# Attention and ReGLU feed-forward on one core: one queue for batch 0's loads, weight rounding on GpSimd alone, and a shorter wait for the value products

## The chip and the metric

One NeuronCore of a Trainium2 chip runs the whole kernel. The time is the device time of one execution in microseconds. Before the change the median of three runs is 424.37 us (424.24 to 425.08). A profile is one further execution, recorded instruction by instruction. TensorE (PE) multiplies matrices, VectorE (DVE), ScalarE (ACT) and GpSimd (POOL) work elementwise, and SyncE (SP) only issues transfers. Each engine runs its own instructions in order, and semaphores hold an instruction until what it needs is there.

## What is computed

Eight batches of eight heads, 576 query rows, 16 extra "beacon" keys in front of 576 keys, 64 elements a head. Causal softmax attention is followed by a feed-forward block with a ReLU gate over all 4608 rows:

```python
k_all = concatenate([beacon_k, k], axis=2)          # 8, 8, 592, 64
v_all = concatenate([beacon_v, v], axis=2)
scores = q @ k_all.T / 8, masked causally behind the beacons
a = exp(scores - max) / sum
x = (a @ v_all) as 4608 x 512
out = (maximum(x @ w_gate, 0) * (x @ w_val)) @ w_out  # 512 -> 1536 -> 512
```

## The kernel before

**A planner writes the order.** The kernel does not issue work in loop order. `Plan.add` (L132) collects tasks, each with an engine (or several to choose from), a modelled cost, what it depends on, which buffers it holds and a priority. `Plan.order` (L140) then simulates all engines and repeatedly starts the task that can begin earliest; ties go by priority. Only after that are the instructions emitted, in that order. So a changed cost, priority or limit can move instructions everywhere. A task that lists two engines, such as `("ACT", "DVE")`, is given to the one that could begin it first. `Hold` and `Slots` stand for buffers that are taken and given back; `Share` limits how many buffers of a common pool one kind of task may hold.

**Loads and preparation of a batch** (`new_batch`, L415). For each of the four head pairs there is one k and one q load of 512 rows (`load_pair`, L451). The remaining 64 rows of k with the 16 beacon rows, and the first 64 and the last 16 rows of q, are the *rest* pieces: one tile of 80 rows for k and one for q, each by two transfers of many short runs (`load_rest`, L487). v comes in five tiles of up to 128 rows (`load_v`, L524). Every load lands in one of `N_ST` = 7 staging tiles `st`. `rounded` (L423) casts it to bf16 into one of three tiles `h16` (L429), on POOL, or for batch 0 on POOL or DVE; `turned` (L434) transposes it on PE against the identity (L441) into PSUM; an eviction copies it on ACT (L386) or DVE (L388) into `kT` or `diag`. `diag` is a block layout of q that must be zero elsewhere: the first two batches' `diag` tiles are cleared once by `make_zeros` (L368), one on DVE and one on POOL. The letters of `ORDER0` (L541) give the order of batch 0's loads: `K` and `Q` the rest pieces, `0` to `3` the pair loads (first k, then q), `v` the v tiles. Batch 0's rest pieces are issued from ACT's queue (`ACT_B` = 1, L497 and L500), everything else from SP's.

**Attention** (`group`, L652, and `tile_step`, L556). For each pair: scores on PE (L602, L594), mask and row minimum on DVE (L617, L614; the scores carry a minus sign), exponential with row sum on ACT (L628), the reciprocal on DVE (L640), the normalisation of the bf16 weights `pa` and `pb` (L647) on POOL (batch 0: POOL or DVE). The weights are then transposed into `pTa` and `pTb`: on PE for batch 0 (L685), by transfers of SP's queue otherwise (L695). The value products (L706, L728) write two PSUM tiles a pair and group, which are copied to `xT`. The scores of batch b are not planned before `PACE` = 39 us times b.

**Values in runs.** The value matmuls use halves or quarters of PE's array, and the planner charges `SWITCH` for going in and out of that mode (`part=True`). Their task carries `lazy` (L734): as long as PE is not in the mode and fewer than `LAZY` us have passed since the product was ready, other PE work that could begin at the same time goes first (L178). So several products gather into one run.

**PSUM banks.** Eight banks are shared (L306 to L308). Scores may hold `SC_MOST` = 4 of them, the feed-forward block `F_MOST` = 3, and values together with the turns of batch 1 and later `V_MOST` = 4.

**Weights.** 36 tiles of 128x512 f32 (12 of each matrix) are loaded by SP into `osb` staging tiles (L401; a pool of `N_OSB` = 6 that the output uses later) and rounded to bf16 by the engine that the planner picks out of `WCAST`, POOL (L390) or ACT (L386).

**Feed-forward** (`ffn`, L755). Spans of 240, 336, then 512 rows and a last one of 448: twelve blocks of a gate product (L764), ReLU on ACT (L775), a value product (L769) and the multiplication on DVE (L779); then the output product in three parts (L792), a copy to `osb` and a store by SP (L802). It needs the `xT` rows of its span and the weights, and fills PE wherever attention leaves room.

Of the kernel before, what the change touches and what calls it, by code (L numbers as in the profile page):

```python
# [25 lines left out]
FILL_FROM = 6.0  # L26
SWITCH = 0.1
LAGS = {"PE": 0.22, "ACT": 0.16, "DVE": 0.14, "POOL": 0.1, "DMA": 0.1}
LAZY = 22.0
LAZY1 = 0.0  # L30
SLOT_LAZY = 0
ON_PE = 1
NORM_B = 1
WCAST = ('POOL', 'ACT')
F_MOST = 3
SC_MOST = 4
SC_FIRST = 6
V_MOST = 4
OUT = -1300.0
ACT_B = 1  # L40
ORDER0 = 'KQ00112233vvvvv'
N_ST = 7
N_OSB = 6
FIRST_SPANS = [240, 336]
# [7 lines left out]
class Slots:  # L52


    def __init__(self, tiles):
        self.free = [(0.0, i, t) for i, t in enumerate(tiles)]
# [41 lines left out]


class Task:  # L100
    def __init__(self, engines, cost, run, deps, holds, prio, lag, part=False, lazy=0.0, move=0.0):
        self.part, self.lazy, self.move = part, lazy, move
        self.engines, self.cost, self.run, self.holds = engines, cost, run, holds
        self.prio, self.lag = prio, lag
        self.deps = [d for d in deps if d is not None]
        self.left = len(self.deps)
        self.users = []
        self.ready = 0.0
        self.start = None
# [14 lines left out]
class Plan:  # L124
# [4 lines left out]
        self.backlog = backlog  # L129
        self.filled = 0.0  # L130

    def add(self, engines, cost, run, deps=(), holds=(), prio=0.0, lag=None, part=False, lazy=0.0, after=0.0, move=0.0):  # L132
        t = Task(engines if isinstance(engines, tuple) else (engines,), cost, run, deps, holds, prio, lag, part, lazy, move)
        t.ready = after
        for d in t.deps:
            d.users.append(t)
        self.tasks.append(t)
        return t

    def order(self):  # L140
        free = {}
        queue = {}
        for t in self.tasks:
            for e in t.engines:
                free.setdefault(e, 0.0)
                queue.setdefault(e, [])
        for t in self.tasks:
            if t.left == 0:
                for e in t.engines:
                    queue[e].append(t)  # L150
        wire = 0.0
        part = False
        free["DMA"] = 0.8
        done = []

        def begin(t, e):
            at = t.ready
            if e == "DMA":
                at = max(at, wire - self.backlog)
            for h in t.holds:  # L160
                if h.tile is None:
                    first = h.slots.first(sum(x.tile is None and x.slots is h.slots for x in t.holds) - 1)
                    if first is None:
                        return None
                    at = max(at, first)
            return max(at, free[e]), at

        while True:
            best = None
            for e in queue:  # L170
                for t in queue[e]:
                    times = begin(t, e)
                    if times is None:
                        continue
                    at, could = times
                    late = 0
                    if e == "PE":
                        late = -1 if part and t.part else 1 if not part and at < (could if SLOT_LAZY else t.ready) + t.lazy else 0  # L178
                    key = (at, late, t.prio)
                    if best is None or key < best[0]:  # L180
                        best = (key, t, e)
            if best is None:
                break
            (at, _, _), t, e = best
            for x in t.engines:
                queue[x].remove(t)
            for h in t.holds:
                if h.tile is None:
                    h.tile = h.slots.take()
            if e == "PE" and FILL_FROM < free[e] and at < self.filled:  # L190
                for tiles in self.fillers:
                    spare = [f for f in tiles.free if f[0] <= free[e]]
                    if spare:
                        n = int((at - free[e]) * FILL / (0.215 if at > 13.0 else 0.5))
                        if n > 0:
                            done.append(Filler(n, spare[-1][2], self.fill))
                        break
            t.start, t.engine = at, e
            cost = t.cost
            if e == "DMA":  # L200
                issue, move = cost
                if issue > 1.2:
                    wire = max(wire, at + 0.3) + move
                    free[e] = max(at + issue, wire - 0.2)
                else:
                    free[e] = at + issue
                    wire = max(wire, at + issue) + move
                end = max(wire, free[e]) + 1.9
            else:
                if isinstance(cost, dict):  # L210
                    cost = cost[e]
                if e == "PE":
                    cost += SWITCH * (t.part != part)
                    part = t.part
                free[e] = end = at + cost
                if t.move:
                    wire = max(wire, end) + t.move
                    end = wire + 1.9
            for h in t.holds:
                h.users -= 1  # L220
                if h.users == 0:
                    h.slots.give(end + (0.1 if e == "DMA" else LAGS[e] if t.lag is None else t.lag), h.tile)
            done.append(t)
            for u in t.users:
                u.ready = max(u.ready, end + (LAGS[e] if t.lag is None else t.lag))
                u.left -= 1
                if u.left == 0:
                    for x in u.engines:
                        queue[x].append(u)
        assert all(t.start is not None for t in self.tasks)  # L230
        self.end = max(free.values())
        return done
# [3 lines left out]
def kernel(  # L236
# [12 lines left out]
    nc = tc.nc  # L249
# [118 lines left out]
    def make_zeros(i):  # L368
        def run(x):
            (nc.vector if x.engine == "DVE" else nc.gpsimd).memset(diag_t[i].bitcast(FP32), 0.0)  # L370

        return run
# [2 lines left out]
    on_mask = add("POOL", 0.9, make_mask, prio=-99)  # L375
    on_zeros = {}
    for i, e in enumerate(["DVE", "POOL"]):
        on_zeros[i] = add(e, 2.6, make_zeros(i), prio=-98 if i == 0 else -19.9)
    on_sel = add("POOL", 2.0, make_sel, prio=-19.84)
    on_mask_f = add("DVE", 0.9, make_mask_f, (on_sel,), prio=-19.84)  # L380
    on_pads = [add("DVE", 0.05 * len(where), make_pads(t, where), prio=-19.2, after=5.0)
# [25 lines left out]
    def heads(src, b, s0, sl):  # L407
        return src[b, :, s0:s0 + sl, :].rearrange("h s d -> s h d")
# [6 lines left out]
    def new_batch(b, prio, work):  # L415
# [71 lines left out]
        def load_rest(kind, prio):  # L487

            st = Hold(stage_s, 2)
            pieces = {"k": [(k, MAIN, REST), (beacon_k, 0, Nb)], "q": [(q, 0, 64), (q, S - TAIL, TAIL)]}[kind]  # L490
            rows = sum(x[2] for x in pieces)

            def fetch(_):
                s3 = st.tile.rearrange("p (h d) -> p h d", h=H)
                at = 0
                for src, s0, n in pieces:
                    (nc.scalar if b < ACT_B else nc.sync).dma_start(s3[at:at + n], heads(src, b, s0, n))  # L497
                    at += n

            if b < ACT_B:  # L500
                ld = add("ACT", 1.3, fetch, (), (st,), prio[0], 0.1, move=0.72)
            else:
                ld = add("DMA", (1.1, 0.72), fetch, (), (st,), prio[0])
            dst = t.kT if kind == "k" else t.diag
            h16, ca = rounded(dst, st, rows, neg_scale if kind == "q" else 1.0, prio, ld, lambda t_: t_)
            ps, tu = turned(h16, rows, ca, prio, 1)
            zeros = on_zeros.get(b) if kind == "q" else None

            def evict(x):
                ps3 = ps.tile.rearrange("p (a n) -> p a n", a=NP)  # L510
                if kind == "k":
                    copy(x.engine, dst.tile[:, :, Nb + MAIN:], ps3[:, :, :REST])
                    copy(x.engine, dst.tile[:, :, :Nb], ps3[:, :, REST:rows])
                    return
                for hh in range(2):
                    r = slice(64 * hh, 64 * hh + 64)
                    a = NQ * P + TAIL * hh
                    copy(x.engine, dst.tile[r, :, 64 * hh + Nb:64 * hh + 64], ps3[r, :, :64 - Nb])
                    copy(x.engine, dst.tile[r, :, a:a + TAIL], ps3[r, :, 64:rows])

            t.rows[kind, "rest"] = [add(("ACT", "DVE"), {"ACT": 0.6 if kind == "k" else 0.65, "DVE": 0.65 if kind == "k" else 0.75},
                                        evict, (tu, zeros), (ps, dst), prio[1])]
# [354 lines left out]
```

## Time and profile before

| what | us |
|---|---|
| median of three runs | 424.37 |
| the profiled execution, whole time | 427.04 |
| its span, first to last instruction | 425.3 |
| first gate matmul (L764) starts | 40.47 |
| last output matmuls (L792) start | 411.8 |
| chain that ended last: share of PE | 68% |
| the same: DVE, ACT, DMA, POOL | 14%, 6%, 4%, 3% |
| weight casts on POOL: wg, wv, wo | 9, 10, 7 of 0.62 us |
| weight casts on ACT: wg, wv, wo | 3, 2, 5 of 0.62 to 0.68 us |
| mean granted PE clock | 0.98 |

The span is what the profiler sees between the first and the last instruction; the whole time has 1.7 us more around it. A chain of waits is followed back from the last instruction to whatever released each step, so its shares say which engine's work sets the end. An engine's busy share over the whole span mixes three stages: the loads (to some 12 us), attention mixed with feed-forward (to some 350 us), and feed-forward alone. For a change in the first stage, the windows and the timeline of that stage matter.

### The profile page before, as it was taken

To read this page: it belongs to the slowest core of one execution; us is meant where nothing else is said; L and a number is where in the kernel's file an instruction comes from. 1 tells how busy PE (TensorE), PEld (TensorE's weight loads), DVE (VectorE), ACT (ScalarE), POOL (GpSimd) and SP (SyncE) were. 2 spreads that over 40 slices of the span, in tenths; PEclk is the share of its full clock that TensorE was granted. 3 is DMA by queue.
4 is the path that set the end of the run, shared out by engine and by line. 5 is a ranking of instruction groups with operands and counts; after the bars stand their busy time and mean duration, and the time that the engine had idled before them with its cause. 6 is when DMAs were issued, how large, how long until landed. Compare 5 with 4: busy or idle time off the path is not lost.

```text
span 425.3 us, 9480 instructions
## 1 busy us (share of the span) xinstructions
PE 395.1 (93%) x2868; PEld 217.4 (51%) x2903; DVE 322.6 (76%) x1136; ACT 289.1 (68%) x929; POOL 234.0 (55%) x433
## 2 busy tenths in 40 slices
PE   0677989999899999999999998999999999999996
PEld 0445776655454554555455544645445444444543
DVE  3899999999889889899899888888885352432432
ACT  2689898877897789798898689978875330330320
POOL 4477889676787677678776677875554000000000
PEclk9957999999999999999999999999999999999999
DMA  8979899979999999999989899974945601101102
GB/s 227 239 212 291 267 258 284 259 147 193 219 244 189 234 222 197 236 208 217 192 242 201 176 214 234 184 159 100 169 77 106 148 2 49 52 0 49 51 0 86
DMA packets 172531, 72.67 MB, mean 171 GB/s; under 512 B 146816, under 2 KB 163328, under 8 KB 172480
## 3 DMA queue, kind: packets, MB, share of 16 engines
q1 hardware_dynamic: 171136, 71.75, 75.7%
q10 hardware_dynamic: 1344, 0.33, 0.4%
q8 instruction: 22, 0.36, 0.4%
q14 instruction: 29, 0.24, 0.2%
HBM read 38.54 MB, written 9.44 MB: 113 GB/s over the span
## 4 chain that ended last, share of the span: by engine, by line
PE 68%; DVE 14%; ACT 6%; DMA 4%; issue 4%; POOL 3%; SPq 0%; POOLq 0%; DVEq 0%; ACTq 0%
PE f L769 18%; PE f L764 18%; PE f L792 17%; PE f L602 5%; DVE f L617 4%; PE f L706 4%; DVE diag L388 2%; ACT pb L628 2%; PE f L441 2%; POOL pb L647 2%; DMA pTb<-pb 2%; DVE hT L779 2%; PE f L594 1%; ACT diag L386 1%; DVE small L617 1%
## 5 line engine op out<-in xcount | busy, mean ns | idle before, releaser
L647 POOL TENSOR_SCALAR pb<-pb,small 128x320 bf16<-128x320 bf16 (+8 forms) x265 | 139.1, 541 | 71.0 <-DVE small L640 57.4
L628 ACT ACTIVATE pb<-f,small 128x448 bf16<-128x448 f32 (+5 forms) x304 | 152.4, 519 | 23.1 <-DVE small L617 13.6
L617 DVE CUSTOM_DVE_ANT_0 f<-f,mask 128x64 f32<-128x64 f32 (+7 forms) x256 | 112.0, 478 | 9.2 <-PE f L602 4.8
L775 ACT ACTIVATE g<-f 128x512 f32<-128x512 f32 (+3 forms) x120 | 66.0, 560 | 71.3 <-PE f L764 68.3
L769 PE MATMUL f<-xT,wv_r 128*128 128x512 bf16 (+3 forms) x472 | 107.5, 360 | 1.1 <-DVE hT L779 0.3
L764 PE MATMUL f<-xT,wg_r 128*128 128x512 bf16 (+3 forms) x467 | 105.8, 360 | 1.6 <-DVE hT L779 0.6
L779 DVE TENSOR_TENSOR hT<-g,f 128x512 bf16<-128x512 f32 (+3 forms) x120 | 75.2, 631 | 41.6 <-PE f L769 36.8
L792 PE MATMUL f<-wo_r,hT 128*128 128x512 bf16 (+3 forms) x442 | 102.9, 373 | 0.8 <-issue 0.2
L764 PEld LDWEIGHTS <-wg_r 128*128 128x128 bf16 x480 | 46.2, 99 | 44.7 <-issue 2.0
L769 PEld LDWEIGHTS <-wv_r 128*128 128x128 bf16 x480 | 45.6, 99 | 42.6 <-issue 2.0
L792 PEld LDWEIGHTS <-hT 128*128 128x128 bf16 (+2 forms) x456 | 43.9, 100 | 44.2 <-issue 1.3
L628 ACT ACTIVATION_READ_ACCUMULATOR pb<-f,small 128x1 f32 x304 | 65.7, 216 | 0.0
L429 POOL TENSOR_SCALAR h<-st 128x512 bf16<-128x512 f32 (+1 forms) x76 | 46.5, 619 | 10.9 <-DVE h L429 2.8
L602 PE MATMUL f<-kT,diag 128*128 128x64 bf16 (+7 forms) x256 | 49.7, 299 | 1.9 <-ACT pa L628 0.9
L441 PE MATMUL f<-ident,h 128*128 128x128 bf16 (+1 forms) x320 | 29.8, 225 | 15.4 <-DVE h L429 9.7
L388 DVE COPY osb<-f 128x512 f32<-128x512 f32 (+3 forms) x32 | 21.5, 672 | 26.6 <-PE f L792 26.2
L617 DVE DVE_READ_ACCUMULATOR2_ANT small<- 128x1 f32 x296 | 41.3, 140 | 0.2
L441 PEld LDWEIGHTS <-h 128*128 128x128 bf16 (+1 forms) x320 | 22.3, 102 | 26.1 <-DVE h L429 10.2
L602 PEld LDWEIGHTS <-diag 128*128 128x128 bf16 x256 | 21.3, 101 | 19.5 <-issue 2.1
L386 ACT CAST diag<-f 64x512 bf16<-64x512 f32 (+2 forms) x48 | 23.4, 499 | 8.9 <-PE f L441 3.6
L706 PEld LDWEIGHTS <-v 128*64 128x64 bf16 (+1 forms) x512 | 21.8, 111 | 12.8 <-issue 9.7
L614 DVE TENSOR_REDUCE small<-f 128x1 f32<-128x512 f32 x40 | 27.3, 681 | 1.0 <-PE f L594 0.8
(60 smaller groups left out, 315.5 us busy)
## 6 DMA issues: line engine op xcount, KB each, us to landing
out_dram<-osb SPq DMA_DIRECT2D x34, 256.0 KB, 2.3
st<-in_k_dram SPq DMA_DIRECT2D x32, 256.0 KB, 4.2
st<-in_q_dram SPq DMA_DIRECT2D x32, 256.0 KB, 5.0
st<-in_v_dram SPq DMA_DIRECT2D x24, 256.0 KB, 5.1
osb<-in_moe_w_gate_dram SPq DMA_DIRECT2D x12, 256.0 KB, 4.7
osb<-in_moe_w_val_dram SPq DMA_DIRECT2D x12, 256.0 KB, 4.2
osb<-in_moe_w_out_dram SPq DMA_DIRECT2D x12, 256.0 KB, 4.8
st<-in_v_dram SPq DMA_DIRECT2D x8, 224.0 KB, 5.1
```

The source lines that it names most:

```text
L429: e.tensor_scalar(order(h16.tile)[:rows], st.tile[:rows] if rows < P else st.tile.rearrange("p (h j d) -> p h j d", h=2, j=4), by, 1.0, AL ...
L441: nc.tensor.matmul(to, h16.tile[:rows, a * P:(a + 1) * P], ident[:rows, :rows], start=True, stop=True)
L602: nc.tensor.matmul(view(i), t.diag.tile[:, p, j * P:j * P + P], kT[:, p, :n], start=True, stop=True)
L617: nc.vector.tensor_tensor_reduce(out=view(i), in0=view(i), in1=msk, scale=1.0, scalar=small["t"][:, 0:1] if name in "EF" else 3.0e38, op0= ...
L628: nc.scalar.activation(ph.tile.rearrange("p a n -> p (a n)")[:, a:a + n], view(i), AF.Exp, bias=small["t"][:, low:low + 1], scale=-1.0, ac ...
L647: (nc.gpsimd if x.engine == "POOL" else nc.vector).tensor_scalar(one, one, small["t"][:, 8 + i:9 + i], 1.0, ALU.mult, ALU.mult)
L706: nc.tensor.matmul(ps.tile[64 * hh:64 * hh + 64, d0:d0 + w], t.v.tile[:rows, c, D * h:D * h + D], rhs(64 * hh), start=(c == 0), stop=(c == ...
L764: nc.tensor.matmul(psg.tile[:, :mt], wg_r[:, ki, nf * P:(nf + 1) * P], xT[:, ki, m0:m0 + mt], start=(ki == 0), stop=(ki == KM - 1))
L769: nc.tensor.matmul(psv.tile[:, :mt], wv_r[:, ki, nf * P:(nf + 1) * P], xT[:, ki, m0:m0 + mt], start=(ki == 0), stop=(ki == KM - 1))
L775: r = add("ACT", c_act(mt), lambda _, psg=psg, g=g: nc.scalar.activation(g.tile[:, :mt], psg.tile[:, :mt], AF.Relu), (a,), (psg, g), -1000 ...
L779: hid.append(add("DVE", c_dve(mt), lambda _, psv=psv, g=g, nf=nf: nc.vector.tensor_mul(hT[nf].tile[:, :mt], g.tile[:, :mt], psv.tile[:, :m ...
L792: nc.tensor.matmul(ps.tile[:rows, :w], hT[nf].tile[:, t0:t0 + rows], wo_r[:, nf, n0:n0 + w], start=(nf == 0), stop=(nf == NF - 1))
```

## The change

Constants:

```diff
-LAZY = 22.0
+LAZY = 16.0
-WCAST = ('POOL', 'ACT')
+WCAST = ('POOL',)
-V_MOST = 4
+V_MOST = 3
-ACT_B = 1
-ORDER0 = 'KQ00112233vvvvv'
+ZERO1 = 9.0
+ORDER0 = '00KQ11v2233vvvv'
```

The planner's task loses its `move` parameter, which modelled a transfer issued from an engine's own queue:

```diff
-                if t.move:
-                    wire = max(wire, end) + t.move
-                    end = wire + 1.9
```

The second `diag` tile's clearing is planned with a cost of 2.1 instead of 2.6, a lower priority, and not before 9 us:

```diff
-        on_zeros[i] = add(e, 2.6, make_zeros(i), prio=-98 if i == 0 else -19.9)
+        on_zeros[i] = add(e, 2.6 if i == 0 else 2.1, make_zeros(i), prio=-98 if i == 0 else -17.0, after=0.0 if i == 0 else ZERO1)
```

Batch 0's rest pieces are issued by SP, as in every other batch:

```diff
-                    (nc.scalar if b < ACT_B else nc.sync).dma_start(s3[at:at + n], heads(src, b, s0, n))
+                    nc.sync.dma_start(s3[at:at + n], heads(src, b, s0, n))
...
-            if b < ACT_B:
-                ld = add("ACT", 1.3, fetch, (), (st,), prio[0], 0.1, move=0.72)
-            else:
-                ld = add("DMA", (1.1, 0.72), fetch, (), (st,), prio[0])
+            ld = add("DMA", (1.1, 0.72), fetch, (), (st,), prio[0])
```

So the loads of batch 0 stand in SP's queue as k0, q0, k rest, q rest, k1, q1, the first v tile, the pairs 2 and 3, and the other v tiles. All weights are rounded on POOL. Value products of batch 2 and later (`lazy` is 0 before) wait 16 us at most in the plan, and values and turns hold three banks at most.

More of the change, by code (lines that the diff above doesn't have):

```diff
@@ L100, with __init__ @@
 class Task:
-    def __init__(self, engines, cost, run, deps, holds, prio, lag, part=False, lazy=0.0, move=0.0):
-        self.part, self.lazy, self.move = part, lazy, move
+    def __init__(self, engines, cost, run, deps, holds, prio, lag, part=False, lazy=0.0):
+        self.part, self.lazy = part, lazy
         self.engines, self.cost, self.run, self.holds = engines, cost, run, holds
@@ L130, in __init__, with add @@
         self.filled = 0.0
-    def add(self, engines, cost, run, deps=(), holds=(), prio=0.0, lag=None, part=False, lazy=0.0, after=0.0, move=0.0):
-        t = Task(engines if isinstance(engines, tuple) else (engines,), cost, run, deps, holds, prio, lag, part, lazy, move)
+    def add(self, engines, cost, run, deps=(), holds=(), prio=0.0, lag=None, part=False, lazy=0.0, after=0.0):
+        t = Task(engines if isinstance(engines, tuple) else (engines,), cost, run, deps, holds, prio, lag, part, lazy)
         t.ready = after
```

## The prediction

> **What bounds the kernel now.** I read the page first, for the engines and the 40 slices.
>
> ```profile
> span 425.3 us, 9480 instructions
> ...
> PE 395.1 (93%) x2868; PEld 217.4 (51%) x2903; DVE 322.6 (76%) x1136; ACT 289.1 (68%) x929; POOL 234.0 (55%) x433
> ...
> PE   0677989999899999999999998999999999999996
> ```
>
> TensorE (PE) is busy 93% of the span, and the first four slices (10.6 us each) are its weak ones. So the time is PE's queue of matmuls plus what PE loses, and most of the loss lies before 60 us. Then I read the windows:
>
> ```profile
> 12.00:20.00 8.00, 5.29 (x38) 3.63 (x37) 6.33 (x25) 5.45 (x18) 4.00 (x7) 1.00 1.13 220
> 20.00:30.00 10.00, 7.29 (x47) 3.76 (x45) 9.93 (x47) 8.28 (x30) 6.60 (x12) 0.51 0.84 234
> 30.00:40.00 10.00, 6.79 (x71) 4.62 (x70) 8.57 (x34) 9.45 (x31) 8.62 (x17) 0.84 0.92 272
> 40.00:50.00 10.00, 9.89 (x89) 7.81 (x89) 9.21 (x30) 8.97 (x30) 7.76 (x13) 0.79 0.87 272
> 50.00:60.00 10.00, 8.11 (x103) 6.42 (x101) 9.92 (x38) 8.88 (x28) 8.93 (x15) 1.00 1.03 284
> 60.00:70.00 10.00, 9.94 (x108) 7.42 (x107) 9.26 (x40) 9.64 (x32) 8.84 (x17) 1.00 1.12 297
> ```
>
> The columns are the length, then busy us of PE, weight loads, DVE, ACT, POOL, then granted clock, DMA share, GB/s. From 20 to 40 us VectorE (DVE) and ScalarE (ACT) are the full ones, with batch 0's softmax. The first gate matmul (L764) starts at 40.47; from there PE is nearly full (8.11 only in 50 to 60). Adding the nine windows of 25 us from 100 to 325, PE is idle 5.2 us in 225. The chain of waits is PE almost alone after 320 us. Whatever starts PE's work earlier moves the end; whatever serves it better after 100 us can win 5.2 us at most. Last the first 14 us of the timeline:
>
> ```profile
> 0.79 0.47 SPq L457 DMA_DIRECT2D st<-in_k_dram  x1
> 0.79 0.71 ACTq L497 DMA_DIRECT2D st<-in_k_dram  x1
> ...
> 2.20 2.12 ACTq L497 DMA_DIRECT2D st<-in_q_dram  x2
> ...
> 7.72 0.62 POOL L429 TENSOR_SCALAR h<-st 128x512 bf16<-128x512 f32 x1 [2.10 <-DMA st<-in_k_dram]
> 10.12 0.42 DVE L429 TENSOR_SCALAR h<-st 80x512 bf16<-80x512 f32 x1 [2.86 <-DMA st<-in_q_dram]
> ...
> 10.60 1.11 PE L441 MATMUL f<-ident,h 80*128 80x80 bf16 x8 [3.12 <-DVE h L429]
> ...
> 11.14 1.28 POOL L429 TENSOR_SCALAR h<-st 128x512 bf16<-128x512 f32 x2 [2.80 <-DVE h L429]
> ...
> 13.33 0.66 PE L602 MATMUL f<-kT,diag 128*128 128x128 bf16 x3 [0.71 <-DVE diag L388]
> ```
>
> The q rest piece, on ACT's queue, is issued from 2.20 and landed only at 10.1, because the five pair loads on SP's queue share the 16 engines with it. PE's in-order queue has its turn ahead of pair 0's k turn, so PE stands 3.12 us, and POOL stands 2.80 us behind it for one of three h16 tiles.
>
> **The change, part by part.**
>
> **One queue, pair 0 first.** SP now issues k0, q0, k rest (2 DMAs), q rest (2), k1, q1. Prices: 0.47 each for the pairs (above); for the rest pieces batch 1's own on SP, 0.94 + 0.34 + 1.29. From 0.79 the q rest is issued by 0.79 + 0.94 + 1.28 + 1.29 = 4.30. Its second piece starts near 3.7; batch 1's equals land after 2.9 to 3.4 us, so 6.6 to 7.1. The other way: 832 KB at the first slices' 227 to 239 GB/s is 3.6 us after some 3.3 us for the first issue and the shortest landing (2.7), so 6.9. I take 7.2, which is 2.9 earlier than 10.1. Behind it stands what stood before: cast, turn, evictions, 2.24 us from 10.12 to the first score at 12.36. The other three scores of the pair then waited until 13.33 for q0's second eviction, which now is done early: 13.33 becomes 9.5, a gain up to 3.8. DVE's first mask-and-minimum (13.82) moves with it, and DVE is the stage's limit. Pairs 1 to 3 gain nothing in landing and lose 2.57 us of SP issue, but they are cast by 17.0 and pair 3's first scores run at 28.85: over 10 us of cover. The v tile moved ahead of pairs 2 and 3 (2 DMAs, 0.41 + 0.42 of issue) hides in the same cover; its product is only due at 23.8. ACT loses four issues (3.46 us) at a time when it had nothing to do. Value **-3.0**, since the full DVE stretch starts later (16.2) and may give some back; ends -0.5 (the landing gain is eaten by the 10 us that already lie between landing and use) and -3.8.
>
> **Second zero memset after 9 us.** POOL's 2.07 us at 2.48 moves behind the first casts, so POOL is free at 3.6 for k0. Queued behind it then are casts of pairs 1 to 3, with the same 10 us of cover. **0**; without that cover it is +2.07.
>
> **Weights on POOL alone.** 10 of the 36 casts run on ACT now (3 wg, 2 wv, 5 wo, between 29.6 and 69.8; 0.62 to 0.68 each, 6.3 us in sum). On POOL they are 10 x 0.62 = 6.2 us, and POOL is idle 1.38 + 2.24 + 1.07 + 1.16 = 5.85 us from 30 to 70. So they just fill it. Queued behind a cast on POOL are batch 1's normalisations (only POOL may do them), behind those SP's transposes (SP waited 92.8 us for L647 over the run), behind those all loads. ACT gets 6.3 us at a time when it shares the chain with DVE. DVE also pays: its bf16 normalisation of 128x64 took 0.45 us and of 128x256 0.28 us, so the smaller took longer, beside a POOL that was casting (four of them 1.88 us at 25.14, beside L390 casts). At up to 0.27 us each for some 10 such instructions that is 2.7. Ends -0.7 (one ACT cast off the path) and +5.8 (2.7 and the 3.1 us by which five wo casts end later); I take **+0.5**, as the row nearest is the idle POOL time that nearly holds them.
>
> The Trainium skill, GPSIMD Engine Reference, Specifications, says that GpSimd's SBUF interfaces are shared with VectorE, with contention for VectorE's two-port modes. The trace agrees (0.45 beside 0.28 us), and by that rule alone the term would be the +2.7.
>
> **Values wait 16 instead of 22, in three banks.** Runs of value matmuls: one group alone is 0.81 us (79.89 to 80.70), three together 2.19; a run costs about 0.15 us before and 0.15 us behind in drained PE, so 0.3. I count 12 runs for the 24 groups of batches 2 to 7. Groups come 39/4 = 9.75 us apart in the plan, so a wait of 22 gathers three, one of 16 two: about 3 to 4 more runs, +1.0. With at most two groups (four PSUM tiles) a third bank is freed in time by evictions of 0.36 to 0.49 us, while a pair of tiles takes PE 0.73. A pT tile comes free earlier: SP's transposes waited 7.3 us for L706, but PE waited under 1 us for transposes. Ends -1.5 (part of the 5.2 us) and +3.6 (all 24 groups alone). **+1.0**.
>
> The `move` parameter goes, which changes only the plan.
>
> **Sum**: -3.0 + 0 + 0.5 + 1.0 = -1.5. The profiled execution took 427.04 (span 425.3), so 425.5 (span 423.8); the median of the runs is 2.67 below the profiled one, so **422.9**.
>
> **Rivals.**
>
> *POOL becomes the bound, slower.* Place: POOL from 30 to 75 us. For it: 6.2 us asked, 5.85 free, SP's queue behind it. Against: ACT and DVE can take other work over, and POOL has 7.4 us free from 12 to 30 for what comes earlier. Price +5.8, so -3.0 + 5.8 + 1.0 = +3.8: 428.2. It decides from a term of 2.0 on. Chance 0.27.
>
> *Values broken up, slower.* Runs of one group, +3.6: -3.0 + 0.5 + 3.6 = +1.1: 425.5. For it: three banks against six tiles in a run of three groups. Against: the due times still gather two. Chance 0.11.
>
> *The start is hidden.* Half of it comes through: -1.5 + 0.5 + 1.0 = 0: 424.4. For it: DMA is full from 12 to 20 (share 1.13), and pair 3's scores run 12 us after its casts. Against: the scores of pair 0 are what DVE waits for. Also here: a new plan that gathers values as before. Chance 0.14.
>
> *The clock comes up sooner, faster still.* PE's granted clock is 0.50 in the 2 us windows from 38 to 44, while the first gates run; PE was busy 3.98 of 4 us from 40 to 44, so full speed there, with its edges (0.83 and 0.96 in the windows beside), is worth some 2.2 us: -3.7: 420.7. Against: PE has the same gaps between 12 and 36. Chance 0.11.
>
> The Trainium skill, TensorE: Matmul & The Clock Gate, What's actually happening, says that the clock halves after an idle window of about 3.4 us and returns after a busy one. The trace agrees in part: four 128x128 turns took 0.63 us at 13.78, after the idle start, and 0.38 at 18.42; but it halved again at 20.3 without such a gap. By that rule an earlier start of PE would favour the last rival.
>
> **Chances and range.** The forecast has 0.37. Faster by over 0.2% (0.85 us, what a measurement can tell from no change): 0.37 + 0.11 = 0.48. Within: 0.14. Slower: 0.27 + 0.11 = 0.38. The forecast's own range is 421.3 to 423.5. Over all cases 420.2 to 428.3 leaves about one in ten on each side.
>
> **What would show it.** Right: q rest cast before 8 us, first scores before 10.5, no 3 us gap of PE behind a cast; the first gate at 37 to 38.5; POOL at 95% from 30 to 70 with PE still full from 60; 14 to 16 value runs for batches 2 to 7. Wrong: the first gate still at 40 (the start was hidden), PE idle over 2 us between 50 and 80 behind wo casts (POOL), or more than 20 value runs. The forecast fails if PE's idle time after 60 us grows by more than the start gives.

## The result, and the profile after

The changed kernel takes 426.64 us (median of 6 runs, 425.79 to 427.30), the kernel before 424.31 (6 runs, 423.75 to 425.08). The ratio is 1.0052, 95% interval 1.0036 to 1.0068: slower by some 2.3 us, where 1.5 us faster was forecast.

The two spans are nearly equal (425.1 after, 425.3 before), because the profiled execution of the kernel before was a long one (427.04 against a median of 424.31), while that of the changed kernel (426.83) is near its median. So stages are compared here, not spans. First the page of the changed kernel:

```profile
span 425.1 us, 9481 instructions
...
PE 398.6 (94%) x2900; PEld 217.4 (51%) x2900; DVE 325.6 (77%) x1128; ACT 284.4 (67%) x928; POOL 238.9 (56%) x442
...
PE   4478897999999999999999999999999999999996
```

PE begins a slice earlier than before (4 and 4 in the first two slices, 0 and 6 before), and has a new dent, the 7 in slice 7 (64 to 74 us). The windows of the changed kernel, with the columns as before (length, busy us of PE, weight loads, DVE, ACT, POOL, granted clock, DMA share, GB/s), show both:

```profile
20.00:30.00 10.00, 7.06 (x40) 3.16 (x39) 9.21 (x37) 7.30 (x30) 8.23 (x15) 0.50 0.93 265
30.00:40.00 10.00, 9.23 (x91) 7.08 (x90) 9.62 (x37) 9.86 (x34) 7.27 (x13) 0.78 1.04 313
40.00:50.00 10.00, 8.17 (x98) 6.51 (x98) 9.79 (x32) 8.57 (x27) 9.66 (x17) 1.00 0.96 272
...
60.00:70.00 10.00, 7.84 (x57) 4.86 (x55) 9.28 (x26) 5.75 (x19) 9.39 (x18) 1.00 0.85 257
70.00:80.00 10.00, 9.31 (x54) 5.59 (x54) 8.52 (x35) 7.40 (x29) 6.58 (x13) 0.83 0.73 139
```

From 30 to 40 us PE works 9.23 us instead of 6.79: the feed-forward block began earlier. From 60 to 70 it works 7.84 instead of 9.94, ACT 5.75 instead of 9.64, while DVE and POOL look busy. The timeline of the first 9 us of the changed kernel:

```profile
3.27 1.28 SPq L494 DMA_DIRECT2D st<-in_q_dram  x2
...
6.66 0.61 POOL L426 TENSOR_SCALAR h<-st 80x512 bf16<-80x512 f32 x1 [0.52 <-PE f L438]
...
8.77 1.33 PE L596 MATMUL f<-kT,diag 128*128 128x64 bf16 x6
```

The q rest piece is cast at 6.66 (10.12 before), and the first scores run at 8.77 (12.36 and 13.33 before). The 3 us gap of PE behind that cast is gone; a shorter one, 2.18 us behind a later cast, stands at 13.13. The first gate product starts at 37.26 instead of 40.47. Then, between 64 and 71 us of the same timeline:

```profile
64.66 0.63 POOL L641 TENSOR_SCALAR pb<-pb,small 128x448 bf16<-128x448 bf16 x1
...
64.91 3.98 DVE L629 TENSOR_TENSOR small<-small 128x1 f32<-128x1 f32 x1
...
65.27 2.36 POOL L387 TENSOR_SCALAR wo_r<-osb 128x512 bf16<-128x512 f32 x4
...
67.61 0.69 POOL L641 TENSOR_SCALAR pb<-pb,small 128x512 bf16<-128x512 bf16 x1
68.27 0.61 POOL L387 TENSOR_SCALAR wo_r<-osb 128x512 bf16<-128x512 f32 x1
68.81 0.42 DVE L611 CUSTOM_DVE_ANT_0 f<-f,mask 128x256 f32<-128x256 f32 x1
...
70.15 0.49 DVE L773 TENSOR_TENSOR hT<-g,f 128x336 bf16<-128x336 f32 x1
...
70.69 0.41 PE L588 MATMUL f<-kT,diag 128*128 128x512 bf16 x2 [2.85 <-DVE hT L773]
```

The line to learn from is L629 (L635 before). It adds the two row sums of an E or F step: two numbers a partition, 0.14 us where nothing disturbs it. Here it lasts 3.98 us, and it ends at 68.89, when POOL's unbroken row of instructions ends (68.27 + 0.61 = 68.88). A bar that long for two numbers a partition suggests a wait; e1 below tests it. DVE's queue stood behind it, so ACT had no scores to exponentiate, PE's next product waited 2.85 us for a multiplication at 70.15 on DVE, and PE's clock then halved:

```profile
68.00:70.00 2.00, 0.00 (x0) 0.00 (x0) 2.00 (x7) 0.67 (x3) 1.40 (x3) 1.00 0.10 20
70.00:72.00 2.00, 1.31 (x9) 0.73 (x9) 1.39 (x6) 1.31 (x6) 1.41 (x5) 0.97 0.22 43
72.00:74.00 2.00, 2.00 (x6) 1.00 (x5) 2.00 (x7) 1.73 (x5) 1.98 (x4) 0.50 1.34 103
74.00:76.00 2.00, 2.00 (x12) 1.16 (x11) 1.14 (x4) 1.07 (x4) 0.00 (x0) 0.67 1.23 280
```

These are windows of 2 us of the changed kernel. The half clock from 72 to 75 costs 1.0 + 0.66 = 1.7 us more. The longest such add in the kernel before:

```profile
88.08 1.26 DVE L635 TENSOR_TENSOR small<-small 128x1 f32<-128x1 f32 x1
88.14 1.20 POOL L390 TENSOR_SCALAR v<-st 128x512 bf16<-128x512 f32 x2
```

It too ends with the row on POOL (88.14 + 1.20 = 89.34 = 88.08 + 1.26). So the mark stood in the trace before.

Nor are these two alone. In the five traces that keep the two-operand add (both kernels, and e2 to e4 below) 36 of the adds last over 0.5 us, and 35 of them end within 0.013 us of the end of a GpSimd instruction. In some of them the next GpSimd instruction follows without a gap, so the add sometimes gets in between two, and sometimes, as here, only behind the row.

### The profile page after: what moved, and what is told of

Read it like the earlier page. It is cut to its first block, busy times and chain, and to the rows that moved or that the text cites. A ratio compares the mean times of both kernels' runs of the same rounds, so it can differ in the third digit from the quotient of the medians.

```text
span 425.1 us, 9481 instructions
## 1 busy us (share of the span) xinstructions
PE 398.6 (94%) x2900; PEld 217.4 (51%) x2900; DVE 325.6 (77%) x1128; ACT 284.4 (67%) x928; POOL 238.9 (56%) x442
## 4 chain that ended last, share of the span: by engine, by line
PE 76%; DVE 14%; ACT 4%; issue 2%; DMA 2%; POOL 1%; SPq 1%; DVEq 0%; POOLq 0%; ACTq 0%
PE f L786 20%; PE f L763 20%; PE f L758 19%; PE f L596 6%; PE f L700 4%; DVE f L611 4%; PE f L438 3%; DVE diag L385 2%; DVE small L629 2%; PE f L588 1%; DVE hT L773 1%; DMA st<-in_q_dram 1%; ACT pb L622 1%; PE f L679 1%; DVE small L611 1%
## 5 line engine op out<-in xcount | busy, mean ns | idle before, releaser
L641 POOL TENSOR_SCALAR pb<-pb,small 128x320 bf16<-128x320 bf16 (+8 forms) x262 | 136.2, 536 | 70.6 <-DVE small L634 60.7
L611 DVE CUSTOM_DVE_ANT_0 f<-f,mask 128x384 f32<-128x384 f32 (+7 forms) x256 | 111.4, 478 | 7.2 <-PE f L596 5.1
L769 ACT ACTIVATE g<-f 128x512 f32<-128x512 f32 (+3 forms) x120 | 66.9, 560 | 72.9 <-PE f L758 72.3
L763 PE MATMUL f<-xT,wv_r 128*128 128x512 bf16 (+3 forms) x480 | 108.6, 359 | 0.7 <-ACT diag L383 0.3
L786 PE MATMUL f<-wo_r,hT 128*128 128x512 bf16 (+2 forms) x456 | 106.2, 377 | 0.2 <-DVE osb L385 0.2
L622 ACT ACTIVATION_READ_ACCUMULATOR pb<-f,small 128x1 f32 x304 | 64.7, 213 | 0.0
L426 POOL TENSOR_SCALAR h<-st 128x512 bf16<-128x512 f32 (+1 forms) x79 | 48.2, 618 | 6.1 <-DMA st<-in_q_dram 2.8
L596 PE MATMUL f<-kT,diag 128*128 128x384 bf16 (+7 forms) x256 | 49.0, 299 | 2.1 <-ACT diag L383 0.9
L385 DVE COPY osb<-f 128x512 f32<-128x512 f32 (+2 forms) x33 | 22.2, 672 | 26.0 <-PE f L786 25.3
L385 DVE CAST diag<-f 64x512 bf16<-64x512 f32 (+2 forms) x44 | 24.8, 574 | 4.1 <-ACT diag L383 3.7
```

What stands on the lines that cost most here:

```text
L385: nc.vector.tensor_copy(dst, src)
L426: e.tensor_scalar(order(h16.tile)[:rows], st.tile[:rows] if rows < P else st.tile.rearrange("p (h j d) -> p h j d", h=2, j=4), by, 1.0, AL ...
L596: nc.tensor.matmul(view(i), t.diag.tile[:, p, j * P:j * P + P], kT[:, p, :n], start=True, stop=True)
L611: nc.vector.tensor_tensor_reduce(out=view(i), in0=view(i), in1=msk, scale=1.0, scalar=small["t"][:, 0:1] if name in "EF" else 3.0e38, op0= ...
L622: nc.scalar.activation(ph.tile.rearrange("p a n -> p (a n)")[:, a:a + n], view(i), AF.Exp, bias=small["t"][:, low:low + 1], scale=-1.0, ac ...
L641: (nc.gpsimd if x.engine == "POOL" else nc.vector).tensor_scalar(one, one, small["t"][:, 8 + i:9 + i], 1.0, ALU.mult, ALU.mult)
```

## The experiments

Theory A: the add's two operands in SBUF come through a port that VectorE shares with GpSimd, and a row of casts on GpSimd holds it up. The Trainium skill, GPSIMD Engine Reference, Specifications, names such contention for VectorE instructions "with two SBUF inputs"; the trace agrees and gives its size, 3.98 for 0.14 us. Theory B: GpSimd's own queue is late. Theory C: the value products cost it. Theory D: the early start is lost on the way. Theory E: it is lost at the hand-over, where PE runs out of feed-forward work and has to wait for batch 1.

All runs together; the marks are from each kernel's trace (us from the span's start), the last mark being the first gate product of 512 columns (the third span of the feed-forward block), which needs batch 1's last values:

| kernel | median | first scores | first gate | first 512-column gate | span |
|---|---|---|---|---|---|
| before | 424.3 to 424.8 | 12.36 | 40.47 | 106.38 | 425.3 |
| changed | 426.64 | 8.77 | 37.26 | 108.08 | 425.1 |
| e1: changed, one-operand sum | 418.78 | 9.47 | 38.34 | 103.78 | 418.6 |
| e2: changed, casts on ACT too | 433.29 | 9.79 | 40.66 | 114.42 | 432.0 |
| e3: before, casts on POOL alone | 427.05 | 11.83 | 44.62 | 107.34 | 425.2 |
| e4: before, start changed | 430.19 | 8.95 | 38.27 | 112.15 | 427.2 |
| e5: before, one-operand sum | 422.83 | 12.28 | 40.40 | 104.00 | 421.5 |
| e6: e1, wait 22 and four banks | 418.94 | 8.85 | 36.99 | 102.17 | 416.5 |
| e7: e3, one-operand sum | 422.85 | 11.65 | 44.42 | 106.46 | 421.1 |
| e8: e2, one-operand sum | 431.17 | 9.77 | 40.60 | 115.47 | 432.1 |
| e9: e1, wo casts on ACT too | 422.15 | 8.76 | 36.85 | 103.14 | 420.0 |
| e10: e1, wg and wv casts on ACT too | 422.42 | 9.71 | 40.63 | 107.54 | 422.3 |
| e11: e1, rest pieces first | 422.61 | 10.40 | 38.24 | 106.50 | 421.3 |

Two cautions on the table. The spans are of one profiled execution each, some of them long or short ones: 427.04 us for a median of 424.31 before, 420.32 for 418.78 in e1, 428.90 for 430.19 in e4, 433.82 for 431.17 in e8. And e1 and e6 have the same order on all engines up to 128 us, yet their marks differ by 0.6, 1.35 and 1.6 us; smaller differences between marks mean nothing.

From the 512-column gate to the end of the span all thirteen take 314.3 to 318.9 us, while the gate itself comes between 102.17 and 115.47. So most of the difference between kernels is made before that gate, and up to 4.6 us of it behind. At the gate PE has done the feed-forward work of batch 0's rows and can only go on with batch 1's last values; this is the hand-over meant below.

**e1, the add with one operand.** The row sums stand in neighbouring columns, so a reduction does the same. The planned cost is the same, and in the two traces the order of the instructions on all five engines is the same, apart from this one's form:

```diff
-            sums = [add("DVE", 0.08, lambda _: nc.vector.tensor_tensor(
-                out=small["t"][:, 4:5], in0=small["t"][:, 4:5], in1=small["t"][:, 5:6], op=ALU.add), sums, (), prio, 0.18)]
+            sums = [add("DVE", 0.08, lambda _: nc.vector.tensor_reduce(
+                out=small["t"][:, 6:7], in_=small["t"][:, 4:6], axis=AX.X, op=ALU.add), sums, (), prio, 0.18)]
...
-            nc.vector.reciprocal(small["t"][:, 8:8 + len(whole)], small["t"][:, 4:4 + len(whole)])
+            at = 6 if name in "EF" else 4
+            nc.vector.reciprocal(small["t"][:, 8:8 + len(whole)], small["t"][:, at:at + len(whole)])
```

> The changed kernel, with the add of the two row sums (one VectorE instruction with two operands in SBUF, 40 times) written as a reduction over the two neighbouring columns, so one operand; planned cost and so the whole order stay as they are. Theory A (shared port): in the changed kernel's trace this add stood 3.98 us at 64.91, until GpSimd's back-to-back row of normalisations and weight casts ended at 68.88; PE then had nothing for 2.85 us and ran at half clock from 72 to 75, which is worth 1.7 us more. With one operand it takes under 0.3 us each time, PE has no gap over 1 us at 67 to 71, and the time is 426.6 - 4.5 = about 422. Theory B (GpSimd's queue itself is late with wo, whoever waits): the add gets short but PE waits for wo casts or normalisations instead, 426 to 427. Theory C (values in three banks): no change, 426.6.

Measured: 418.78 us, ratio to the kernel before 0.9847 (0.9810 to 0.9883), 7.9 us under the changed kernel; their intervals, 0.7 and 1.6 us either way, leave no doubt of it. Of the 6.5 us between the two spans, 4.3 lie before the 512-column gate (103.78 against 108.08), about what the stall and the half clock cost (2.85 + 1.7). The same place in its timeline:

```profile
65.75 0.15 DVE L629 TENSOR_REDUCE small<-small 128x1 f32<-128x2 f32 x1
...
66.08 2.37 POOL L387 TENSOR_SCALAR wo_r<-osb 128x512 bf16<-128x512 f32 x4
...
68.42 0.69 POOL L642 TENSOR_SCALAR pb<-pb,small 128x512 bf16<-128x512 bf16 x1
...
68.52 0.41 PE L588 MATMUL f<-kT,diag 128*128 128x512 bf16 x2
...
69.08 0.62 POOL L387 TENSOR_SCALAR wo_r<-osb 128x512 bf16<-128x512 f32 x1
69.67 3.30 POOL L642 TENSOR_SCALAR pb<-pb,small 128x576 bf16<-128x576 bf16 x7
```

The same casts stand in a row on POOL, the sum takes 0.15 us, and PE's product L588 runs in step. Theory A holds: with this one instruction changed, stall and loss are gone. (The reduction is also another operation, and it writes a column of its own instead of its first operand; no run separates that from the second operand.) More than the one stall went: the groups of the two kernels, by shape, say that the 40 sums took 16.0 us of DVE in the changed kernel and 6.0 in e1.

```profile
L629 DVE TENSOR_TENSOR small<-small 128x1 f32<-128x1 f32 x40 | 16.0, 400 | 2.8 <-ACT pb L622 1.5 <-ACT pa L622 1.1
```

```profile
L629 DVE TENSOR_REDUCE small<-small 128x1 f32<-128x2 f32 x40 | 6.0, 149 | 2.6 <-ACT pb L622 1.2 <-ACT pa L622 1.1
```

(Columns: busy us and mean ns, then the idle time before.) Theory B falls by e1's windows:

```profile
60.00:70.00 10.00, 10.00 (x74) 6.28 (x72) 8.08 (x36) 8.13 (x29) 10.00 (x20) 1.00 0.98 280
70.00:80.00 10.00, 9.89 (x91) 6.39 (x90) 9.53 (x38) 9.47 (x35) 10.00 (x21) 1.00 1.01 191
```

POOL is busy without a break from 60 to 80 us, and PE is full all the same.

**e2, the changed kernel with casts on ScalarE again.**

```diff
-WCAST = ('POOL',)
+WCAST = ('POOL', 'ACT')
```

> The changed kernel with weight casts on GpSimd or ScalarE again, the rest of the change kept. Theory A: the row of casts on GpSimd is broken up, no add over 1.5 us, 421.5 to 423. Theory B: the same time, but with an add of any length; GpSimd below 90% busy from 30 to 70. Theory C (the loss is from the value products): still 426 to 427.

Measured: 433.29, ratio 1.0192 (1.0155 to 1.0229). A miss for all theories: no sum stood longer than 0.66 us, and yet it is the slowest of all. PE's loss lies between 105 and 120 us, where it has no feed-forward work left: the first 512-column gate came at 114.42.

**e3, the kernel before with casts on GpSimd alone.**

```diff
-WCAST = ('POOL', 'ACT')
+WCAST = ('POOL',)
```

> The kernel before with weight casts on GpSimd alone. Theory A: it costs what the longest add or normalisation costs that meets a row of casts on GpSimd; 424 where none does, up to 429 where one does, and the trace tells which. Theory B: 426 to 430 whatever the adds do. Theory C: 424 to 425.

Measured: 427.05, ratio 1.0056 (1.0033 to 1.0078). The trace has sums of 1.49 (twice) and 1.13 us. Either A or B could do that; e7 tells.

**e4, the kernel before with the start alone.**

```diff
-ACT_B = 1
-ORDER0 = 'KQ00112233vvvvv'
+ACT_B = 0
+ZERO1 = 9.0
+ORDER0 = '00KQ11v2233vvvv'
...
-        on_zeros[i] = add(e, 2.6, make_zeros(i), prio=-98 if i == 0 else -19.9)
+        on_zeros[i] = add(e, 2.6 if i == 0 else 2.1, make_zeros(i), prio=-98 if i == 0 else -17.0, after=0.0 if i == 0 else ZERO1)
```

> The kernel before with the first loads alone changed: one queue, first pair in front of the rest pieces, second zero memset after 9 us; casts, wait and banks as before. If the 3.2 us by which the changed kernel's first gate product starts earlier carry through to the end: 421 to 422. If they are lost on the way without any help from casts and values (theory D: VectorE, ScalarE or DMA hide the start): 424 to 425.

Measured: 430.19, ratio 1.0115 (1.0079 to 1.0152), outside both expectations. The early start is there (scores at 8.95, first gate at 38.27), and it is lost at the hand-over: the 512-column gate came at 112.15, 5.8 us later than before, with PE busy 19.5 of 25 us from 100 to 125 (23.6 before). An earlier start of feed-forward makes it run out earlier; here batch 1 moreover came later than before, and no run says why.

**e5, the kernel before with the one-operand sum** (the edit of e1).

> The kernel before with the one-operand sum alone, order unchanged. Its adds took 11.7 us in sum against 6.0 at 0.15 each, the longest 1.26. Theory A (the stall on the shared port is a price that the change brought): little to win here, 423 to 424.5. Theory A' (the port costs both kernels about the same and the changed one is slower for another reason): 417 to 419, as much as in the changed kernel.

Measured: 422.83, ratio 0.9965 (0.9947 to 0.9983). The two-operand add costs the kernel before 1.9 us, the changed one 7.9. So some 6 us of it came with the change.

**e6, e1 with the value products as before.**

```diff
-LAZY = 16.0
+LAZY = 22.0
-V_MOST = 3
+V_MOST = 4
```

> The changed kernel with the one-operand sum (418.8) and the value products put back: wait 22, four banks. If the shorter wait and the third bank cost what the prediction said (+1.0, up to 3.6): 415 to 418. If they serve PE: 419 to 425, with the first 512-column gate product, which needs batch 1's last values, later than 103.8.

Measured: 418.94, ratio 0.9858 (0.9840 to 0.9876), against 418.78 and 0.9847 with the short wait. No difference: theory C falls, and the +1.0 of the prediction with it, in the kernel without the stall.

**e7, e3 with the one-operand sum** (the edits of e3 and e1).

> The kernel before with weight casts on GpSimd alone (427.05) and the one-operand sum. Theory A (casts on GpSimd cost through the port): 423 to 424.5, the sums 0.15 each. Theory B (they cost GpSimd's own time): still 426 to 427.

Measured: 422.85, ratio 0.9957 (0.9941 to 0.9973), the same as e5 (422.83). With the one-operand sum, moving ten casts to GpSimd costs nothing; with two operands, 427.05 - 424.62 = 2.4 us. B is out here too.

**e8, e2 with the one-operand sum** (the edits of e2 and e1).

> The changed kernel with the one-operand sum, and weight casts on GpSimd or ScalarE (433.3 with the add of two operands). Theory E: what is lost there is the hand-over at batch 1: PE ran out of feed-forward work and the first 512-column gate product came at 114 to 118 instead of 103.8, since ScalarE's casts delay batch 0 and 1's attention; the port has no part in it, so 431 to 433.5. Theory A (port in this one too): 419 to 425.

Measured: 431.17, ratio 1.0156 (1.0132 to 1.0180). As theory E expects: the add is worth only 2.1 us here (433.29 - 431.17), and the hand-over comes at 115.47. So there are four pairs of kernels that differ by the form of the add alone:

| kernel | casts | two operands | one operand | price of the add |
|---|---|---|---|---|
| before (e5) | GpSimd and ScalarE | 424.73 | 422.83 | 1.9 |
| e3 (e7) | GpSimd alone | 427.05 | 422.85 | 4.2 |
| e2 (e8) | GpSimd and ScalarE, changed start and values | 433.29 | 431.17 | 2.1 |
| changed (e1) | GpSimd alone, changed start and values | 426.64 | 418.78 | 7.9 |

The price is high where GpSimd has all the casts, and higher still in the changed kernel's order. The windows of e8:

```profile
90.00:100.00 10.00, 10.00 (x91) 5.58 (x89) 8.71 (x37) 6.57 (x24) 4.99 (x11) 1.00 0.77 139
100.00:110.00 10.00, 7.90 (x64) 4.30 (x63) 9.10 (x36) 7.67 (x32) 8.34 (x16) 0.89 1.13 241
110.00:120.00 10.00, 6.46 (x69) 3.77 (x68) 7.68 (x38) 8.10 (x29) 7.40 (x14) 0.94 0.83 169
```

From 90 to 100 PE is full of the last feed-forward work while POOL, which batch 1's normalisations need, is half idle (4.99); after that PE stands.

**e9 and e10, which casts on ScalarE do it.** e1, with ScalarE allowed for wo alone (it took 6 of 12), or for wg and wv alone (it took 2 of each 12):

```diff
-            WCAST, {"DVE": 0.4, "ACT": 0.52, "POOL": 0.6},
+            ("POOL", "ACT") if kind == "o" else WCAST, {"DVE": 0.4, "ACT": 0.52, "POOL": 0.6},
```

```diff
-            WCAST, {"DVE": 0.4, "ACT": 0.52, "POOL": 0.6},
+            WCAST if kind == "o" else ("POOL", "ACT"), {"DVE": 0.4, "ACT": 0.52, "POOL": 0.6},
```

> The changed kernel with the one-operand sum, where only the 12 wo tiles may go to ScalarE; wg and wv stay on GpSimd. With no cast on ScalarE it took 418.8, with all allowed 431.2. Theory E1 (casts on ScalarE at 30 to 50 us delay batch 0 and 1's attention): the first 512-column gate product near 104 and 418 to 421. Theory E2 (the wo casts at 60 to 70 do it, or any change of the order there): 111 to 118 and 425 to 433.

> The changed kernel with the one-operand sum, where only wg and wv tiles may go to ScalarE and wo stays on GpSimd. Theory E1: the first 512-column gate product at 111 to 118 and 427 to 433. Theory E2: near 104 and 418 to 422.

Measured: 422.15 (0.9939, 0.9916 to 0.9961) and 422.42 (0.9944, 0.9926 to 0.9963). Each time misses both of its expectations: neither alone makes the 12.4 us between e1 and e8; they cost 3.4 and 3.6. With wg and wv on ScalarE the first gate comes at 40.63 instead of 38.34, so there the casts do delay the start, as E1 says, though the hand-over (107.54) comes earlier than E1 has it; with wo on ScalarE the hand-over is in time (103.14), and PE loses 1.4 us in the 25 us from 100 (23.48 busy, 24.86 in e1). Why both together cost over three times as much stays open, and so does theory E's reason for the late hand-over: every such edit makes the planner write a new order.

**e11, e1 with the rest pieces first.**

```diff
-ORDER0 = '00KQ11v2233vvvv'
+ORDER0 = 'KQ0011v2233vvvv'
```

> The changed kernel with the one-operand sum and the rest pieces in front of pair 0, still on one queue. If it is the single queue that brings the early start: first scores within 1 us of 8.8, 418 to 420. If it is the first pair's place: first scores at 10 to 12 and the first gate product 1 to 3 us later, 420 to 423.

Measured: 422.61, ratio 0.9949 (0.9924 to 0.9974). First scores at 10.40, against 8.76 to 9.47 in the changed kernel, e1, e6 and e9, which have one order up to there; the first gate is no later (38.24), but the hand-over comes at 106.50. At the first scores more than half of the gain (12.36 to 10.40) comes with the single queue and the rest with the pair's place. At the end it is otherwise: e11 is 0.2 us faster than e7 (422.85), which has the old start, and e1 another 3.8. Nearly all that the start gives needs pair 0 in front.

## Why the prediction was wrong

*What bounds the kernel.* Right that PE's lost time lies early. But the runs put the point that decides at about 105 us, where batch 1 hands over. It was not in the prediction, and a gain at the start can be lost there (e4: -3.4 us at the first scores, +5.6 at the end).

*One queue, pair 0 first, -3.0.* Right at the start: q rest cast at 6.66 (landing estimated at 7.2), first scores 8.77 (9.5), first gate 3.2 us earlier. To the end it carries -3.9 us, from e7 (422.85) to e6 (418.94), which differ by the start alone. But only with the casts on GpSimd: with ScalarE taking some it costs 5.6 (e4), and 8.3 from e5 (422.83) to e8 (431.17), where the add has one operand and the values differ too. That condition was missing, so the size that came out owes something to luck. The rival of the hidden start was thus right about a kernel that was not the one predicted.

*Second memset, 0.* It ran on POOL at 9.30 for 2.07 us and nothing in the marks shows a cost; not tried alone.

*Weights on POOL alone, +0.5.* This is the step that failed. It was priced as GpSimd's time and as slower bf16 normalisations on VectorE, with the queue behind GpSimd as the risk. The casts' time on GpSimd costs nothing net (e7 against e5: 0.0), and VectorE's normalisations hardly changed (19 with 8.1 us busy before, 22 with 9.7 after). What the unbroken row of casts does is hold up VectorE's 128x1 add with two operands, an instruction that was in no term: 1.9 us before (e5), 7.9 after (e1), so +6.0 in place of +0.5. The casts alone account for 2.4 of it (e3); the rest appears only together with the new order of start and values. Contention was thought of, and applied to the wrong instruction. The rival with the bound on GpSimd had about the right price (+5.8) for the wrong mechanism: in e1 GpSimd is busy without a break from 60 to 80 us and PE full. Of the prediction's signs those of the start came true, and PE full from 60 us did not. The sign of a loss, PE idle over 2 us between 50 and 80, showed too, but PE stood behind VectorE's add, not behind wo casts.

*Values, +1.0.* The count was right (14 or 15 runs for batches 2 to 7, 10 to 12 before, by how neighbouring runs are counted), the price was not: e6 and e1 differ by 0.2 us, the other way and within the noise. The 0.3 us of drained time that was charged per run is shown by no run; by the prediction's own rows three runs of one group (3 x 0.81) take 0.24 us more than one run of three (2.19), which is 0.12 a run.

*The sum* by the measured steps: 424.7 - 1.9 (two-operand add of the kernel before taken out, e5) + 0.0 (casts, e7) - 3.9 (start, e6) - 0.2 (values, e1) = 418.7, then + 7.9 with the add back in: 426.6. Each step is the difference of two measured kernels, so the chain ends at the measured time by construction; what it shows is where the 2.3 us lie. In another order the steps have other sizes (e4).

*The clock* rival: its condition came true in part. In windows of 2 us the granted clock is 1.00 from 36 to 50 us in the changed kernel, so the first gates run at full speed, where it was 0.50 from 38 to 44 before. In return it is 0.50 from 14 to 34, where before it was 0.50 to 0.57 from 20 to 30 and 1.00 again from 32 to 36. No run separates what this is worth.

The version that beats both is the changed kernel with the one-operand sum, with either wait: 418.8 to 418.9 us, 1.4% to 1.5% under the kernel before by the ratios.

## What to carry to other kernels

Before work is moved to GpSimd, list every VectorE instruction with two operands in SBUF, however small: its price can be the row of GpSimd instructions that it meets, and a maximum far over the median (1264 against 158 ns here) in the trace before gives it away. Instructions with one tensor operand need a look too: in the changed kernel VectorE's 128x256 bf16 normalisation took from 0.37 to 1.26 us, the longest at 27.4 us beside casts on GpSimd; no run tested that one. Where two small operands are neighbours, a reduction over both does the same with one operand, and here removed the wait. And follow a gain at the start to the next point where one batch hands over to the next: if what arrives there isn't earlier too, the gain becomes a wait.

## What the runs showed of the hardware

- A 128x1 add with two SBUF operands took 0.14 us at the least and up to 3.98 us beside back-to-back GpSimd instructions. It did not always get in at their boundaries: the longest began inside one and stood through six more. The one-operand reductions took 0.12 to 0.16 us, all 40 in each of the eight kernels that have them, whatever GpSimd did.
- The granted clock of a window can read 1.00 where PE runs at half speed. In e1 and in e6 (one window each):

```profile
28.00:36.00 8.00, 6.88 (x52) 4.62 (x54) 7.97 (x31) 6.27 (x25) 6.29 (x12) 0.50 0.96 290
```

```profile
28.00:36.00 8.00, 7.02 (x65) 5.09 (x67) 7.97 (x33) 6.79 (x25) 6.28 (x12) 1.00 1.06 306
```

The clock reads 0.50 in the one and 1.00 in the other, but the matmuls say otherwise: the 128x384 score product that starts between 30 and 36 us took 512 ns in both, and a mean of 326 ns from 44 us on in both. In e6 every window of 2 us from 12 to 36 us reads 1.00, even where a 128x512 score product took 631 ns, against 379 ns later. So a clock at the start of a trace is to be checked against the duration of a known matmul.

- The first gate comes at 37.26 us in the changed kernel, 38.34 in e1 and 36.99 in e6, with the same order up to there. A single trace of this stage thus carries some 1.4 us of chance.
